# First softmax in halves, half of a halo mask and one weight cast moved to GpSimd, and four columns summed by TensorE alone, in the start of a fused dynamic convolution and max-out feed-forward kernel

## Chip, cores and metric

The kernel runs on one core of a Trainium2 chip. The metric is the device time of one execution in microseconds (us). The engines are called by the profile's names: PE is TensorE (PEld its weight loads), DVE is VectorE, ACT is ScalarE, POOL is GpSimd, SP is SyncE, which here only issues DMAs.

## What is computed

The input x is 8 x 4160 tokens of 192 numbers (33280 tokens in all), in 8 heads of 24. A causal convolution over 7 tokens has a softmax of its own for every token and head; its result goes through a max-out layer of width 1024.

```python
def _attn_ref(x, weight_gen):            # weight_gen: B, S, 8 heads, 7 taps
    w = np.exp(weight_gen - max over taps)
    w = w / (np.sum(w, axis=-1, keepdims=True) + 1e-09)
    x_pad = 6 zero tokens ahead of each sequence
    return einsum('bshk,bskhg->bshg', w, x_unf)      # 7 neighbouring tokens
...
h1 = x @ w1                               # 192 -> 1024
h2 = x @ w2
g = np.maximum(h1, h2)
return g @ w_out                          # 1024 -> 192
```

## The kernel before

**Layout.** Each of the 128 partitions holds 260 consecutive tokens, here called columns. Sixteen columns make a batch (17 batches, the last with 4 columns). Batches 0 and 1 are cut into pieces of 4 columns, later ones into pieces of 8. A piece is a unit of the feed-forward part.

**Softmax of a batch.** `load_wg` loads the 7 x 8 raw weights of each column. `exp_sum` (ACT, L127) takes the exponential, `red` (DVE, L139) sums over the taps, `ln` (ACT, L142) takes the logarithm of the sum, `shift` (DVE, L147) subtracts it from the raw weights, and `weights` (ACT, L158) takes the exponential again, which is the normalised softmax, into `en_t` in bf16, every value twice.

**Convolution of a piece.** `mul` (DVE, L173) multiplies seven shifted copies of x with the weights into `m_t` (7 taps side by side). For batches 2 and later, `adds` has three DVE additions (L189, L195, L198) that leave the sum in `y_t`; a DMA transposes it into `yt`. For the first eight units (batches 0 and 1) the sum over taps and the transposition are done on PE: `sum_transpose(u)` (L239) multiplies the taps with an identity and accumulates them in PSUM, and ACT copies the result into `yt` (L246). With all 7 taps that is 84 matmuls. Where the DVE has first done the first of its additions, `adds(b, o, True)`, four tiles `LEFT` are left and it is 48 matmuls. Units 0, 1 and 3 have all seven taps; units 2 and 4 to 7 are of the LEFT kind.

**Feed-forward.** The max-out is computed as h1 + relu(h2 - h1). `w_diff` (DVE subtractions L551 and L555, and three copies into other partitions by an engine that it is given) makes the difference of the two weights in two halves. `hid_tile` (PE, L275) makes a tile of the hidden layer, `relu` (ACT, L285) rectifies it into `rd_t`, and PE multiplies with `moe_w_out` (L315). The h1 part is folded: w1 is transposed on PE (`w1_transposed`, L580, from the bf16 copies `w1E` of rows 0 to 127 and `w1T` of rows 128 to 191), copied by ACT (L640), multiplied with w_out (`w10_product`, L622) and copied (`w10_copies`, L634); PE then adds `yt` times that product to the output (L327). ACT evacuates it (L371) and SP stores it.

**The start.** Everything is issued in a hand-written order; each engine runs its own instructions in that order. x for columns 0 to 7 and the weights come by SP's queue in f32. The six tokens ahead of each partition's first one (the halo, 1152 numbers) come in two DMAs, of SP and of POOL; where a sequence begins, the halo is zeroed by a multiplication with the mask `msk`, on ACT (L536). x of columns 0 to 3 is cast by DVE (L540), of columns 4 to 7 by ACT (L547). POOL copies one number per partition as a gate (L560), so that its own loads start only after the first halves of the weights have landed; then come its loads of x and w_out. `load_x(1, 0, 8)` issues the load of batch 1's first 8 columns and then a DMA (L121) that copies the last six columns of batch 0 to batch 1's halo; it waits for columns 12 to 15 of batch 0. PE runs 30 dummy matmuls (`keep_warm`, L592) until the first `sum_transpose`.

**Later.** From batch 2 on, `transpose(u)` issues the DMA transpose, and POOL copies one number of its result into `gate` (L215) ahead of its next loads. DVE runs a batch or two ahead of PE.

Of the kernel before, what the change touches and what calls it, by code (L numbers as in the profile page):

```python
# [23 lines left out]
def kernel(  # L24
# [83 lines left out]
                        ap=[[CPP * WGC, P], [1, n * WGC]]),  # L108
        )

    def load_x(b, o, n):

        if b not in xb_ts:
            xb_ts[b] = pxb.tile([P, (16 + PAD) * D], BF16, name="xb_t", tag="xb")
        nc.gpsimd.dma_start(  # L115
            out=xb_ts[b][:, (PAD + o) * D:(PAD + o + n) * D],
            in_=bass.AP(tensor=x.tensor, offset=(BATCHES[b][0] + o) * D,
                        ap=[[CPP * D, P], [1, n * D]]),
        )
        if b > 0 and o == 0:  # L120
            nc.gpsimd.dma_start(out=xb_ts[b][:, 0:PAD * D],  # L121
                                in_=xb_ts[b - 1][:, 16 * D:(16 + PAD) * D])


    def exp_sum(b):
        e_ts[b] = pe_.tile([P, BATCHES[b][1] * WGC], FP32, name="e_t", tag="e")
        nc.scalar.activation(out=e_ts[b], in_=wg_ts[b], func=AF.Exp)  # L127

    def part(b, i, of):

        n = BATCHES[b][1]
        h0, h1 = n * i // of * H, n * (i + 1) // of * H
        return slice(h0, h1), h0 * K, [[K, h1 - h0], [1, K]]

    def red(b, i=0, of=1):
        if i == 0:
            s_ts[b] = psm.tile([P, BATCHES[b][1] * H], FP32, name="sum_t", tag="sum")
        hs, at, ap = part(b, i, of)
        nc.vector.reduce_sum(out=s_ts[b][:, hs], in_=_sub(e_ts[b], at, ap), axis=AX.X)  # L139

    def ln(b):
        nc.scalar.activation(out=s_ts[b], in_=s_ts[b], func=AF.Ln)  # L142

    def shift(b, i=0, of=1):
        hs, at, ap = part(b, i, of)
        w_t = _sub(wg_ts[b], at, ap)
        nc.vector.tensor_tensor(out=w_t, in0=w_t, in1=_sub(s_ts[b], hs.start, [[1, hs.stop - hs.start], [0, K]]),  # L147
                                op=ALU.subtract)
# [15 lines left out]
    def mul(b, o):  # L164

        n = dict(pieces(b))[o]
        if n == 4 and b < 2:
            m_out = _sub(m_t, K * o * D, [[64, 2], [P, K * 6], [1, 64]])
            x_in = _sub(xb_ts[b], o * D, [[2 * D, 2], [D, K], [1, 2 * D]])
        else:  # L170
            m_out = m_t[:, K * o * D:K * (o + n) * D]
            x_in = _sub(xb_ts[b], o * D, [[D, K], [1, n * D]])
        nc.vector.tensor_tensor(  # L173
            out=m_out, in0=x_in,
            in1=_sub(en_ts[b], o * WGC * 2, [[2, K * n * H], [0, G // 2], [1, 2]]),
            op=ALU.mult,
        )

    def adds(b, o, first=False, beside=lambda i, of: None):


        w = dict(pieces(b))[o]
        n = w * D

        def taps(at, step, cnt):
            return _sub(m_t, K * o * D + at * n, [[step * n, cnt], [1, w * D]])

        beside(0, 3)
        nc.vector.tensor_tensor(out=taps(0, 1, 3), in0=taps(0, 1, 3), in1=taps(3, 1, 3), op=ALU.add)  # L189
        if first:  # L190
            return
        beside(1, 3)
        if b not in y_ts:
            y_ts[b] = py.tile([P, 16 * D], BF16, name="y_t", tag="y")
        nc.vector.tensor_tensor(out=taps(0, 2, 2), in0=taps(0, 2, 2), in1=taps(1, 5, 2), op=ALU.add)  # L195
        beside(2, 3)

        nc.vector.tensor_tensor(  # L198
            out=_sub(y_ts[b], o * D, [[64, 2], [P, 3 * w // 2], [1, 64]]),
            in0=taps(0, 1, 1), in1=taps(2, 1, 1), op=ALU.add,  # L200
        )
# [28 lines left out]
    def sum_transpose(u, taps=range(K)):  # L230

        b, o, n = UNITS[u]
        assert n == 4
        yps = ps["r" if "r" in ps else "o"].tile([P, 1024], FP32, name="yps", tag="op")
        for k in range(6):
            for t in taps:
                for r in range(2):
                    at = (K * o + t * n) * D + k * P
                    nc.tensor.matmul(  # L239
                        yps[:, r * 512 + k * 64:r * 512 + (k + 1) * 64],  # L240
                        lhsT=m_t[half(r), at:at + P], rhs=ident[half(r), half(r)],
                        start=(k == 0 and t == taps[0]), stop=(t == taps[-1]),
                        skip_group_check=True,
                    )
        yt = pyt.tile([P, 8 // 2 * 3 * P], BF16, name="yt", tag="yt")
        nc.scalar.copy(out=_sub(yt, 0, [[64, 2], [P, 6], [1, 64]]),  # L246
                       in_=_sub(yps, 0, [[512, 2], [64, 6], [1, 64]]))
        yt_ts[u] = yt
# [33 lines left out]
    def relu(rd, t0, n):  # L282

        (hd, at), k = hd_at[t0], rd_at[t0][1]
        nc.scalar.activation(out=rd[:, k * 1024:(k + n) * 1024], in_=hd[:, at:at + n * 1024],  # L285
                             func=AF.Relu)
# [124 lines left out]
    def room(g):  # L411

        t0, n = GROUPS[g]
        if "c" in ps:
            ab = ps["ab"].tile([P, 2048], FP32, name="hd2", tag="ab")
            for t in range(t0, t0 + n - 1):
                hd_at[t] = ab, (t - t0) * 1024
            hd_at[t0 + n - 1] = ps["c"].tile([P, 1024], FP32, name="hd1", tag="c"), 0
        else:
            for t in range(t0, t0 + n):  # L420
                hd_at[t] = ps["h"].tile([P, 1024], FP32, name="hdp", tag="hd"), 0
        rd = prd.tile([P, 3 * 1024], BF16, name="rd_t", tag="rd")
        for t in range(t0, t0 + n):
            rd_at[t] = (rd, t - t0)
        return rd
# [8 lines left out]
    def hidden(g, now=(), between=lambda: None, beside=lambda: None, ahead=lambda: None):  # L434


        t0, n = GROUPS[g]
        rd = room(g)
        for t in range(t0, t0 + n - 1):
            hid_tile(t)  # L440
        if now:
            out_room(now, "ab" if n == 1 and "ab" in ps else None)
            last = out_first(now)
        if len(now) > 2:
            relu(rd, t0, n - 1)
        else:
            for t in range(t0, t0 + n - 1):
                relu(rd, t, 1)
        if now:
            go = relay(last)  # L450
        hid_tile(t0 + n - 1)
        if len(now) > 2:
            beside()
        relu(rd, t0 + n - 1, 1)
        ahead()
        if now:
            out_second(now, go)
            evac(now[0] // 2, len(now) // 2)
        between()
        if len(now) <= 2:  # L460
            beside()
# [25 lines left out]
    with tc.tile_pool(name="pstage", bufs=1) as pstage:  # L487
# [23 lines left out]
        def load_w(h):  # L511
            for kind, r0, nr in (("E", 0, P), ("T", P, 64)):
                for wi, wsrc in enumerate((moe_w1, moe_w2)):
# [14 lines left out]
        nc.vector.tensor_single_scalar(out=msk_i, in_=msk_i, scalar=1, op=ALU.min)  # L528
        nc.vector.tensor_copy(out=msk, in_=msk_i)
        nc.vector.tensor_copy(out=ident, in_=ident_f)  # L530
        exp_sum(0)
        red(0)
        ln(0)
        shift(0)
        xb_ts[0] = pxb.tile([P, (16 + PAD) * D], BF16, name="xb_t", tag="xb")
        nc.scalar.activation(out=xb_ts[0][:, 0:PAD * D], in_=xs[:, 0:PAD * D], func=AF.Copy,  # L536
                             scale=msk[:, 0:1])
        for o in (0, 4, 8, 12):
            weights(0, o)
# [8 lines left out]
        def w_diff(h, copy):  # L548

            c0, c1, c2 = (slice(s * F + h * HF, s * F + (h + 1) * HF) for s in range(3))  # L550
            nc.vector.tensor_tensor(out=wd[:, c0], in0=ws["E", 1][:, c0], in1=ws["E", 0][:, c0],  # L551
                                    op=ALU.subtract)
            copy(out=wd[64:P, c2], in_=wd[0:64, c0])
            copy(out=wd[0:64, c1], in_=wd[64:P, c0])
            nc.vector.tensor_tensor(out=wd[0:64, c2], in0=ws["T", 1][:, c0], in1=ws["T", 0][:, c0],  # L555
                                    op=ALU.subtract)
            copy(out=wd[64:P, c1], in_=wd[0:64, c2])
# [6 lines left out]
            out=wo[:, :].rearrange("p (f d) -> p f d", d=D),  # L564
            in_=bass.AP(tensor=moe_w_out.tensor, offset=0, ap=[[D, P], [P * D, FCH], [1, D]]),
        )
        load_x(1, 0, 8)
        load_wg(2, nc.gpsimd)
        load_x(1, 8, 8)
        load_wg(3, nc.gpsimd)  # L570
# [18 lines left out]
        def keep_warm(times):  # L589

            for _ in range(times):
                nc.tensor.matmul(warm[:, 0:512], lhsT=ident, rhs=_sub(ident, 0, [[0, 4], [1, P]]),  # L592
                                 start=True, stop=True, skip_group_check=True)

        keep_warm(30)
        w_diff(0, nc.scalar.copy)
        sum_transpose(0)
        keep_warm(6)
# [1 line left out]


        nc.scalar.copy(out=w1["E"][:, HF:F], in_=ws["E", 0][:, HF:F])
        hidden(0)
        nc.scalar.copy(out=w1["T"], in_=ws["T", 0])
        w_diff(1, nc.vector.tensor_copy)
        mul(0, 8)
        sum_transpose(1)
        exp_sum(1)
        red(1)
        adds(0, 8, True)  # L610
        hidden(1)
        ln(1)
        shift(1)
# [27 lines left out]
        weights(1, 0)  # L641
        mul(1, 0)
        adds(1, 0, True)
        sum_transpose(2, LEFT)
        load_x(2, 0, 16)
        load_wg(4, nc.gpsimd)
        rd = room(3)
# [138 lines left out]
```

The softmax here doesn't subtract the row's maximum and nothing guards it: scores larger than these inputs give would overflow.

## Time and profile before

| | us |
|---|---|
| median of 7 runs (413.42 to 414.62) | 414.4 |
| the profiled execution, its own time | 414.4 |
| its span, first to last instruction | 412.5 |
| busy in the span: PE / DVE / ACT / POOL | 397.6 / 376.9 / 359.2 / 76.6 |
| granted TensorE clock, mean | 0.998 of full |

A row of the timeline is: start, duration, engine and source line, operation, written tile <- read tiles, shapes as partitions x elements, count, and in brackets the engine's idle time before it with what ended it. Records of neighbouring ACT and DVE instructions overlap by some 0.1 us, so a step in a row of instructions is the difference of two starts. In the list of waits a row gives the total, the count and the longest.

### The profile page before, as it was taken

The numbers are of one execution on the slowest core, as the hardware profiler recorded it, in microseconds if no ns is written. First come the engines' busy times: TensorE is split into PE (matmuls) and PEld (weight loads), VectorE is DVE, ScalarE is ACT, GpSimd is POOL, SyncE is SP. The second block draws the span as 40 slices with busy tenths as digits, with TensorE's granted clock in tenths as the row PEclk, the third lists the DMA queues.
The fourth block names the chain that finished last, engine by engine and source line by source line (L and its number), as shares of the span: only waits on it lengthen the run. The fifth ranks groups of instructions, "written<-read, shape, count | busy, mean of one in ns | idle before, by whom it ended". The sixth has DMA issues, their size and how long they took to land.

```text
span 412.5 us, 15844 instructions
## 1 busy us (share of the span) xinstructions
PE 397.6 (96%) x7276; PEld 316.5 (77%) x7276; DVE 376.9 (91%) x218; ACT 359.2 (87%) x425; POOL 76.6 (19%) x102
## 2 busy tenths in 40 slices
PE   7989999999999999999999999999999999999994
PEld 2678999677777787777777787777777677777794
DVE  5999999999999999999999999999999999999000
ACT  5999998989999988999988999989998888888771
POOL 1510102212211232222012222120122121210000
PEclk9999999999999999999999999999999999999999
DMA  8975535775657885864896497588648748654513
GB/s 242 258 183 159 146 79 133 174 160 140 168 118 162 196 164 129 224 178 101 133 258 162 97 261 178 71 246 185 127 103 239 168 74 228 155 85 144 147 77 118
DMA packets 60242, 65.68 MB, mean 159 GB/s; under 512 B 47601, under 2 KB 48497, under 8 KB 60176
## 3 DMA queue, kind: packets, MB, share of 16 engines
q1 hardware_dynamic: 51904, 40.47, 36.6%
q0 software_dynamic: 8128, 24.11, 28.3%
q8 instruction: 57, 0.93, 0.9%
q10 hardware_dynamic: 144, 0.10, 0.1%
q14 instruction: 9, 0.07, 0.1%
HBM read 35.96 MB, written 25.56 MB: 149 GB/s over the span
## 4 chain that ended last, share of the span: by engine, by line
DVE 69%; PE 17%; ACT 5%; issue 4%; DMA 3%; SPq 1%; DVEq 0%
DVE m_t L173 35%; DVE m_t L189 15%; DVE m_t L195 10%; PE op_ps L315 8%; PE hd L275 6%; DVE sum_t L139 3%; DVE y_t L198 3%; DVE wg_t L147 3%; ACT rd_t L285 2%; DMA ws1T<-in_moe_w_dram 2%; PE op_ps L327 2%; DMA yt<-y_t 1%; ACT yt L246 1%; PE hdp L275 1%; ACT e_t L127 1%
## 5 line engine op out<-in xcount | busy, mean ns | idle before, releaser
L285 ACT ACTIVATE rd_t<-hd 128x1024 bf16<-128x1024 f32 (+1 forms) x206 | 234.7, 1189 | 28.3 <-PE hd L275 26.7
L315 PE MATMUL op_ps<-wo,rd_t 64*128 64x192 bf16 x4160 | 210.6, 243 | 0.1
L315 PEld LDWEIGHTS <-rd_t 64*128 64x128 bf16 x4160 | 180.9, 94 | 15.7 <-ACTq L348 0.3
L275 PE MATMUL hd<-yt,wd 64*128 64x512 bf16 (+1 forms) x1584 | 187.5, 360 | 2.4 <-ACT rd_t L285 1.9
L173 DVE TENSOR_TENSOR m_t<-xb_t,en_t 128x10752 bf16<-128x10752 bf16 (+1 forms) x37 | 187.6, 5071 | 0.3 <-ACT en_t L158 0.3
L275 PEld LDWEIGHTS <-wd 64*128 64x128 bf16 x1776 | 94.3, 94 | 44.6 <-issue 3.9
L215 POOL CAST gate<-yt 128x1 f32<-128x1 bf16 x29 | 41.0, 1414 | 273.3 <-DMA yt<-y_t 273.3
L189 DVE TENSOR_TENSOR m_t<-m_t 128x4608 bf16<-128x4608 bf16 (+1 forms) x34 | 79.6, 2340 | 0.1
L371 ACT COPY o_t<-op_ps 128x384 f32<-128x384 f32 (+1 forms) x99 | 57.2, 590 | 13.8 <-PE op_ps L315 13.6
L327 PE MATMUL op_ps<-w,yt 64*128 64x192 bf16 x780 | 55.5, 243 | 1.4 <-ACT w L634 0.7
L327 PEld LDWEIGHTS <-yt 64*128 64x128 bf16 x780 | 38.4, 94 | 17.7 <-issue 2.2
L195 DVE TENSOR_TENSOR m_t<-m_t 128x3072 bf16<-128x3072 bf16 (+1 forms) x29 | 50.1, 1726 | 0.1
L158 ACT ACTIVATE en_t<-wg_t 128x896 bf16<-128x896 f32 (+2 forms) x45 | 35.2, 818 | 0.0
L198 DVE TENSOR_TENSOR y_t<-m_t 128x1536 bf16<-128x1536 bf16 (+1 forms) x29 | 27.3, 942 | 0.5
L361 DVE COPY o_t<-op_ps 128x192 f32<-128x192 f32 x1 | 0.4, 358 | 25.7 <-ACT o_t L361 25.7
L147 DVE TENSOR_TENSOR wg_t<-wg_t,sum_t 128x280 f32<-128x280 f32 (+4 forms) x45 | 22.0, 489 | 0.4 <-ACT sum_t L142 0.4
L139 DVE TENSOR_REDUCE sum_t<-e_t 128x64 f32<-128x448 f32 (+2 forms) x30 | 19.6, 655 | 2.4 <-ACT e_t L127 2.4
L115 POOL DMA_DIRECT2D xb_t<-in_x_dram x32 | 17.2, 539 | 22.9 <-DVE m_t L173 22.3
L127 ACT ACTIVATE e_t<-wg_t 128x896 f32<-128x896 f32 (+1 forms) x17 | 16.0, 939 | 2.4 <-DMA wg_t<-in_weight_gen_dram 2.4
L285 ACT ACTIVATE rd_t<-hdp 128x1024 bf16<-128x1024 f32 x16 | 15.9, 1033 | 1.0 <-PE hdp L275 1.0
L275 PE MATMUL hdp<-yt,wd 64*128 64x256 bf16 x192 | 12.8, 269 | 0.8 <-ACT rd_t L285 0.5
L592 PE MATMUL warm<-ident 128*128 128x512 bf16 x36 | 10.6, 461 | 3.0 <-DVE ident L530 3.0
(46 smaller groups left out, 75.3 us busy)
## 6 DMA issues: line engine op xcount, KB each, us to landing
out_dram<-o_t SPq DMA_DIRECT2D x28, 768.0 KB, 4.5
xb_t<-in_x_dram POOLq DMA_DIRECT2D x28, 384.0 KB, 4.8
wg_t<-in_weight_gen_dram POOLq DMA_DIRECT2D x14, 448.0 KB, 5.8
xb_t<-xb_t POOLq DMA_DIRECT2D x16, 288.0 KB, 5.0
out_dram<-o_t SPq DMA_DIRECT2D x8, 384.0 KB, 3.0
wg_t<-in_weight_gen_dram SPq DMA_DIRECT2D x2, 448.0 KB, 4.7
xs<-in_x_dram SPq DMA_DIRECT2D x2, 384.0 KB, 6.3
xb_t<-in_x_dram POOLq DMA_DIRECT2D x1, 768.0 KB, 8.6
```

The lines of the kernel that those rows point to most:

```text
L147: nc.vector.tensor_tensor(out=w_t, in0=w_t, in1=_sub(s_ts[b], hs.start, [[1, hs.stop - hs.start], [0, K]]), op=ALU.subtract)
L158: nc.scalar.activation(out=_sub(en_ts[b], (o * WGC + j * N * K) * 2, [[2 * N, K], [2, N], [1, 2]]), in_=_sub(wg_ts[b], (o * H + j * N) * K ...
L173: nc.vector.tensor_tensor(out=m_out, in0=x_in, in1=_sub(en_ts[b], o * WGC * 2, [[2, K * n * H], [0, G // 2], [1, 2]]), op=ALU.mult,)
L189: nc.vector.tensor_tensor(out=taps(0, 1, 3), in0=taps(0, 1, 3), in1=taps(3, 1, 3), op=ALU.add)
L195: nc.vector.tensor_tensor(out=taps(0, 2, 2), in0=taps(0, 2, 2), in1=taps(1, 5, 2), op=ALU.add)
L198: nc.vector.tensor_tensor(out=_sub(y_ts[b], o * D, [[64, 2], [P, 3 * w // 2], [1, 64]]), in0=taps(0, 1, 1), in1=taps(2, 1, 1), op=ALU.add,)
L215: nc.gpsimd.tensor_copy(out=gate, in_=yt[:, 0:1])
L275: nc.tensor.matmul(hid_out(t, f, j), lhsT=wd[half(j), s * F + f * P:s * F + (f + 1) * P], rhs=_sub(yt_ts[u][half(j), :], (s + j) % 3 * P, ...
L285: nc.scalar.activation(out=rd[:, k * 1024:(k + n) * 1024], in_=hd[:, at:at + n * 1024], func=AF.Relu)
L315: return nc.tensor.matmul(op_out(c), lhsT=rd[half(r), k * 1024 + at:k * 1024 + at + P], rhs=wo[half(r), f * D:(f + 1) * D], start=False, s ...
L327: nc.tensor.matmul(op_out(c + j), lhsT=yt_ts[u][half(j), (3 * i + (s + j) % 3) * P:(3 * i + (s + j) % 3 + 1) * P], rhs=w10[half(j), s * D: ...
L371: nc.scalar.copy(out=_sub(o, c % 24 * D, [[D, len(qs)], [h * D, 2], [1, D]]), in_=_sub(tile_, at + (qs[0] - p) * D, [[D, len(qs)], [512, 2 ...
```

## The change

The first batch's softmax runs as two halves of eight columns: `exp_sum`, `red`, `ln` and `shift` are issued twice each. The halo is masked half by POOL (576 of the 1152 numbers) and half by ACT. The cast of w1's last 64 rows (`w1T`, 64 x 1024) goes from ACT to POOL, between the load of batch 1's first columns and the DMA that copies its halo. `adds(0, 8, True)` is dropped and `sum_transpose(2)` sums all seven taps on PE. Three dummy matmuls fewer run in `keep_warm`. The exponential of batch 1 moves between the two relus of `hidden(0)` (which is written out), and `red(1)` moves ahead of `mul(0, 8)`; `w_diff(1)` and `sum_transpose(1)` keep their places on their engines.

```diff
-    def load_x(b, o, n):
+    def load_x(b, o, n, amid=lambda: None):
...
+        amid()
         if b > 0 and o == 0:
             nc.gpsimd.dma_start(out=xb_ts[b][:, 0:PAD * D],
                                 in_=xb_ts[b - 1][:, 16 * D:(16 + PAD) * D])
...
-    def exp_sum(b):
-        e_ts[b] = pe_.tile([P, BATCHES[b][1] * WGC], FP32, name="e_t", tag="e")
-        nc.scalar.activation(out=e_ts[b], in_=wg_ts[b], func=AF.Exp)
+    def exp_sum(b, i=0, of=1):
+        if i == 0:
+            e_ts[b] = pe_.tile([P, BATCHES[b][1] * WGC], FP32, name="e_t", tag="e")
+        w = BATCHES[b][1] * WGC // of
+        nc.scalar.activation(out=e_ts[b][:, i * w:(i + 1) * w], in_=wg_ts[b][:, i * w:(i + 1) * w], func=AF.Exp)
...
-    def ln(b):
-        nc.scalar.activation(out=s_ts[b], in_=s_ts[b], func=AF.Ln)
+    def ln(b, i=0, of=1):
+        s_t = s_ts[b][:, part(b, i, of)[0]]
+        nc.scalar.activation(out=s_t, in_=s_t, func=AF.Ln)
...
-        exp_sum(0)
-        red(0)
-        ln(0)
-        shift(0)
+        for step in (exp_sum, red, ln, shift):
+            for i in range(2):
+                step(0, i, 2)
         xb_ts[0] = pxb.tile([P, (16 + PAD) * D], BF16, name="xb_t", tag="xb")
-        nc.scalar.activation(out=xb_ts[0][:, 0:PAD * D], in_=xs[:, 0:PAD * D], func=AF.Copy,
+        HP = PAD * D // 2
+        nc.gpsimd.tensor_scalar(out=xb_ts[0][:, 0:HP], in0=xs[:, 0:HP], scalar1=msk[:, 0:1], scalar2=None,
+                                op0=ALU.mult)
+        nc.scalar.activation(out=xb_ts[0][:, HP:2 * HP], in_=xs[:, HP:2 * HP], func=AF.Copy,
                              scale=msk[:, 0:1])
...
-        load_x(1, 0, 8)
+        load_x(1, 0, 8, lambda: nc.gpsimd.tensor_copy(out=w1["T"], in_=ws["T", 0]))
...
-        keep_warm(30)
+        keep_warm(27)
...
         nc.scalar.copy(out=w1["E"][:, HF:F], in_=ws["E", 0][:, HF:F])
-        hidden(0)
-        nc.scalar.copy(out=w1["T"], in_=ws["T", 0])
+        rd = room(0)
+        hid_tile(0)
+        relu(rd, 0, 1)
+        exp_sum(1)
+        hid_tile(1)
+        relu(rd, 1, 1)
         w_diff(1, nc.vector.tensor_copy)
+        sum_transpose(1)
+        red(1)
         mul(0, 8)
-        sum_transpose(1)
-        exp_sum(1)
-        red(1)
-        adds(0, 8, True)
         hidden(1)
         ln(1)
         shift(1)
...
-        sum_transpose(2, LEFT)
+        sum_transpose(2)
```

## Prediction

> **What bounds the kernel now.** First the page: PE and DVE are both nearly full.
>
> ```profile
> PE 397.6 (96%) x7276; PEld 316.5 (77%) x7276; DVE 376.9 (91%) x218; ACT 359.2 (87%) x425; POOL 76.6 (19%) x102
> ```
>
> Which of the two sets the end is seen in the chain that ended last. It is DVE's row of operations up to 342 us, one transposing DMA, and then PE alone.
>
> ```profile
> 330.71 5.75 DVE m_t L173
> ...
> 341.74 0.88 DVE y_t L198
> 342.76 4.42 DMA yt<-y_t
> 347.21 0.82 PE hd L275 x6
> ```
>
> The list of waits says how tight that handover is: in the whole run PE waited once for a transposed tile, for 0.4 us.
>
> ```profile
> PE hd L275 <- DMA yt<-y_t: 0.4, 1, 0.4
> ```
>
> In the middle of the run DVE needs 23.66 us for 16 columns (L173 starts at 58.61 and 82.27 in the chain), 1.48 us a column; PE in its tail repeats after 8.64 us for 6 columns (L315 at 352.75, 361.39, 370.02), 1.44 a column. PE starts behind DVE and catches up just before the end. So if the start brings DVE forward by D and PE by E, the end moves by the smaller of D and E + 0.4. Neither alone is enough.
>
> Next the start, on DVE's timeline. From 8.73 us each row begins where the one before it ends: whatever is saved or lost here is kept to 342.
>
> ```profile
> 5.40 1.09 DVE L139 TENSOR_REDUCE sum_t<-e_t 128x128 f32<-128x896 f32 x1 [2.44 <-ACT e_t L127]
> 6.86 1.09 DVE L147 TENSOR_TENSOR wg_t<-wg_t,sum_t 128x896 f32<-128x896 f32 x1 [0.38 <-ACT sum_t L142]
> 7.87 0.55 DVE L540 CAST xb_t<-xs 128x768 bf16<-128x768 f32 x1
> 8.73 2.96 DVE L173 TENSOR_TENSOR m_t<-xb_t,en_t 128x5376 bf16<-128x5376 bf16 x1 [0.30 <-ACT en_t L158]
> ...
> 12.81 2.94 DVE L173 TENSOR_TENSOR m_t<-xb_t,en_t 128x5376 bf16<-128x5376 bf16 x1
> 15.67 0.68 DVE L551 TENSOR_TENSOR wd<-ws1E,ws0E 128x512 bf16<-128x512 f32 x1
> ...
> 21.92 1.35 DVE L189 TENSOR_TENSOR m_t<-m_t 128x2304 bf16<-128x2304 bf16 x1
> 23.18 1.08 DVE L147 TENSOR_TENSOR wg_t<-wg_t,sum_t 128x896 f32<-128x896 f32 x1
> ```
>
> ACT's timeline has the halo mask, the cast that waits for x, and the cast that leaves ACT:
>
> ```profile
> 6.76 1.26 ACT L536 ACTIVATE xb_t<-xs,msk 128x1152 bf16<-128x1152 f32 x1
> ...
> 11.36 0.83 ACT L547 CAST xb_t<-xs 128x768 bf16<-128x768 f32 x1 [0.39 <-DMA xs<-in_x_dram]
> ...
> 17.77 1.03 ACT L604 CAST w1T<-ws0T 64x1024 bf16<-64x1024 f32 x1
> ```
>
> Last, POOL's timeline, with DVE's row of the same time in the second fence. A cast of one number takes 0.18 us where DVE runs a reduction (206.44), but 1.75 where DVE runs a multiplication of two SBUF tensors: it ends 0.05 after it (64.32, 64.27).
>
> ```profile
> 2.09 0.24 POOL masks.py:197 MEMSET ident_f<- 128x128 f32 x1
> 2.40 0.29 POOL masks.py:199 TENSOR_SCALAR_AFFINE_SELECT ident_f<-ident_f 128x128 f32<-128x128 f32 x1
> ...
> 62.57 1.75 POOL L215 CAST gate<-yt 128x1 f32<-128x1 bf16 x1 [16.68 <-DMA yt<-y_t]
> ...
> 206.44 0.18 POOL L215 CAST gate<-yt 128x1 f32<-128x1 bf16 x1 [10.93 <-DMA yt<-y_t]
> ```
>
> ```profile
> 58.52 5.75 DVE L173 TENSOR_TENSOR m_t<-xb_t,en_t 128x10752 bf16<-128x10752 bf16 x1
> ```
>
> **First softmax in halves.** Its weights land at 4.40. ACT's slope is 0.81 ns a number (steps of 0.85 for 896, 0.31 for 224), so half an exponential is a row of 0.58: 4.42 to 5.00, the second to 5.49. A reduction of 448 is a row of 0.61: 5.03 to 5.64, the second from 5.56 to 6.18. The logarithms end at 5.95 and 6.48, both ahead of DVE; the subtractions (0.61 each) run 6.10 to 6.71 and 6.64 to 7.25. Before they ended at 7.95: 0.7 earlier. What is late next is the halo and x: the two halo DMAs landed at 6.36 and 6.73, x of the first columns at 7.45. ACT's half of the mask is 1.26 - 576 x 0.81 ns = 0.79, 6.76 to 7.55; its first two `weights` end at 8.22, so that is the earliest for `mul(0, 0)`.
>
> **POOL's half of the mask.** No row shows a wide cast on POOL. One number costs 0.18; the memset gives 1.08 ns a further number ((0.24 - 0.10) / 127), the affine select 0.86 ((0.29 - 0.18) / 127); I take 0.97, so 576 numbers are 0.74. If all of the select's 0.29 went by size it would be 1.3. It can begin at 6.75, finds DVE in the second subtraction, begins at 7.25 and ends at 7.99. DVE's cast L540 comes next. If POOL holds it up, `mul(0, 0)` starts at 8.47, else at 8.22; gain 0.26 or 0.5, with the slow POOL -0.3. I take 0.26. `mul(0, 4)` also needs L547, whose x lands at 11.34 as before (done 12.19); DVE comes to it at 12.55, so it costs nothing.
>
> **The w1T cast on POOL.** From ACT it takes a step of 0.99 (17.77 to 18.76). On POOL it stands behind the gate, three loads and one of w_out, which ended at 14.23 and will at 13.9; its source landed at 13.66. It meets `mul(0, 4)`, running to 15.49, and waits for that, as the gate rows do. Then it reads 64 x 1024 numbers: 0.18 + 1023 x 0.97 ns = 1.17, bounds 1.06 and, by size alone, 2.3. DVE's next instruction is L551, which reads two SBUF tensors. That POOL waits for such an instruction is shown; that DVE waits for POOL is not, since one number is too short to show it. So the cost to DVE lies between nothing and the whole cast. I take the whole, because what excludes the two from each other in one order is likely to in the other: L551 starts at 16.66 in place of 15.41 (15.67 - 0.26), cost 1.25. The Trainium skill, SBUF - State Buffer, section "Who interferes with whom", speaks against this part of the change in the same sense: a VectorE instruction with two SBUF inputs and a GpSimd instruction that reads SBUF exclude each other for a whole instruction, whichever starts first. By that rule the sum is the one with 1.25; without it, the one with nothing. Behind the cast on POOL's queue stands the halo DMA L121, which waited until 18.81 for columns 12 to 15: cover of over 2 us to the cast's end at 16.66. `w1T` is read on PE near 20.5.
>
> **`adds(0, 8, True)` removed.** DVE's step is 23.18 - 21.92 = 1.26, all on its continuous row. PE's 36 more matmuls cost (1.40 - 0.88) / 36 each by the two L239 rows, 0.52 together, in a stretch where PE idled 2 of 17 us (19 to 36). The three dummies (0.30 each) give back 0.91, ending PE's warm-up near 11.1, ahead of `mul(0, 0)`'s end: no cost.
>
> **The order around it.** `red(1)` now needs `exp_sum(1)`, done about 17.5 between the two relus; DVE comes later in both cases. `ln(1)` stands behind the relus of tiles 2 and 3, near 21.5; `shift(1)` comes at 22.9: no stall.
>
> **Sum for DVE.** 0.26 + 1.26 - 1.25 = 0.27 earlier at `shift(1)` and from there on.
>
> **Sum for PE.** `w_diff(1)` ends at 18.05 + 1.0 = 19.05, and tiles 2 and 3 need it (PE came at 18.55). Tile 2 ends at 19.7, its relu starts at 19.75 (20.31 before); tile 4's relu then waits for PE, 22.05 (22.32). The w1t copies start at 23.85 (24.12), `sum_transpose(2)` starts after `mul(0, 8)` at 22.95 and ends at 24.3, w10 follows tiles 6 and 7 at 25.6 (25.70), its copies end at 29.0 (29.27), and PE goes on 0.25 earlier. E + 0.4 = 0.65 exceeds 0.27, so DVE sets the end. From the profiled 414.4 (span 412.5 and 1.9 around it; also the median of the runs) it is 414.1. A measurement of this kernel tells about 0.2%, 0.8 us, from no change, so this counts as within it.
>
> **Rivals.** *POOL doesn't hold DVE up.* DVE gains 0.5 + 1.26 = 1.75; PE gains what ACT loses of work, 0.99, so E + 0.4 = 1.4 sets the end: 413.0. For it: the gate casts left no trace on DVE's next row. Against: one number is no test.
> *POOL is slow and holds the pair of engines for long; slower.* With 2.3 us for the cast and 1.3 for the mask DVE stands at -0.3 + 1.26 - 2.4 = -1.4: 415.8. With the mask as taken, the change turns to a loss once the cast holds DVE beyond 1.5 us, and beyond 2.35 it is a loss of over 0.8. For it: only tiny POOL casts are timed here. Against: memset and select both show about 1 ns a number.
> *PE's instructions come late.* PE has two stalls of 0.8 us inside `sum_transpose`, at 18.48 and 36.60, that the profile puts down to "issue"; 36 more quick matmuls could add one in PE's start, E = -0.5 and the end near 414.5: no change.
>
> **How the numbers follow.** DVE held up by about 1.2: 0.47, time 413.4 to 414.9 by the bounds of mask and cast (1.06 to 1.8). Not held up: 0.28, 412.7 to 413.3. Slow POOL: 0.18, 415.2 to 416. Late instructions: 0.07. The range 412.7 to 415.5 leaves out most of the slow case. Faster by over 0.2%: the second case and a short cast, 0.34; slower: the slow case and a little, 0.20; within: 0.46.
>
> **What would show it.** Right: a row of POOL for w1T of 1 to 1.3 us beginning or ending where `mul(0, 4)` ends, L551 some 1.2 us later after `mul(0, 4)` than its length says, `shift(1)` near 22.9, PE's transposed-tile wait still there near 347. Wrong: L551 unmoved behind `mul(0, 4)` and `shift(1)` near 21.5 (first rival), a POOL row above 2 us (second), or a PE gap above 0.5 us in 20 to 36 that is new (third).

## The result, and the profile after

The changed kernel takes 412.63 us (median of 22 runs) beside 413.91 for the kernel before (58 runs): the ratio on record is 0.9976 [0.997, 0.9982], a gain of 1.0 us (0.74 to 1.24); the plain difference of the two medians is 1.28. The gain of 0.24% is just over the 0.2% at which the prediction put its border between faster and no change, and the interval (0.18 to 0.30%) takes in that border. On the 414.4 from which the prediction counted, it is 413.4: inside its range, but 0.7 below the forecast. The median itself, 412.63, lies just under the range's lower end of 412.7.

The profiled execution has a span of 410.6. Of the 1.9 us between the two spans, 0.98 stands between the last matmuls of the two kernels, which start at 406.83 and 405.85; the other 0.88 lies behind them, in the final stores (below). The profiled execution of before, 414.4, is one of its longer ones. First the page: the busy times barely moved.

```profile
PE 396.8 (97%) x7309; PEld 316.1 (77%) x7309; DVE 376.6 (92%) x219; ACT 357.9 (87%) x426; POOL 82.9 (20%) x104
```

What moved is the chain that ended last. Before, it was DVE's row up to 342 us; now it is mostly PE, and DVE has 1% of it.

```profile
PE 83%; ACT 10%; issue 3%; DMA 2%; DVE 1%; SPq 1%; DVEq 0%; ACTq 0%
```

DVE's timeline of the changed kernel shows the start (L177 was L173, L557 was L551, L151 was L147):

```profile
8.79 2.96 DVE L177 TENSOR_TENSOR m_t<-xb_t,en_t 128x5376 bf16<-128x5376 bf16 x1 [0.61 <-POOL xb_t L540]
...
15.74 0.68 DVE L557 TENSOR_TENSOR wd<-ws1E,ws0E 128x512 bf16<-128x512 f32 x1
16.45 1.01 DVE L559 COPY wd<-wd 64x512 bf16<-64x512 bf16 x1
17.48 0.29 DVE L560 COPY wd<-wd 64x512 bf16<-64x512 bf16 x1
...
22.70 1.09 DVE L151 TENSOR_TENSOR wg_t<-wg_t,sum_t 128x896 f32<-128x896 f32 x1
```

And POOL's timeline has the two operations that it was given:

```profile
6.80 1.96 POOL L540 TENSOR_SCALAR xb_t<-xs,msk 128x576 bf16<-128x576 f32 x1 [4.09 <-DVE wg_t L151]
...
14.30 3.01 POOL L573 CAST w1T<-ws0T 64x1024 bf16<-64x1024 f32 x1
```

DVE's sum can be read off. The subtractions of the two halves end at 7.16, 0.79 earlier than before, but `mul(0, 0)` starts 0.06 later (8.79, 8.73), since it waits 0.61 for POOL's mask. The copy L559 takes 1.01 where its twin L560 takes 0.29: it was held up for 0.72 by POOL's cast. The cast itself takes 1.03 by itself (e7), so of its 3.01 it spent some 2 waiting for the multiplication and the subtraction ahead of that copy. The removed addition is worth its 1.26. So -0.06 - 0.72 + 1.26 = 0.48, and `shift(1)` does start 0.48 earlier (22.70, 23.18).

PE goes the other way. At 29 us it is 0.51 ahead (its first L331, L327 before, starts at 28.80 and 29.32). But its first long hidden tile starts at 49.49, at 49.14 before: 0.35 later, although DVE is ahead. PE's timeline shows why:

```profile
34.86 0.83 PE L279 MATMUL hdp<-yt,wd 64*128 64x256 bf16 x12 [0.90 <-issue]
```

It stops 0.90 in front of a hidden tile, with nothing outstanding that the profile shows, and ACT idles 1.45 for that tile (its relu starts at 35.73). Before, the stop of 0.74 stood inside `sum_transpose(4)`, where nobody waited for it:

```profile
36.60 0.81 PE L239 MATMUL yps<-ident,m_t 64*128 64x64 bf16 x43 [0.74 <-issue]
```

It is one and the same place. When the matmuls of the PE timeline are counted, 607 of them stand ahead of the stop in both kernels, and the change puts 33 more in the program ahead of that place (36 more of `sum_transpose(2)`, 3 dummies fewer). In the 14 profiles of this document there are 31 stops of PE by "issue" over 0.15 us. All stand behind 223, 351, 479, 607, 991 or 1119 matmuls: 128 apart, or a multiple of it. The page's row for instruction transfers, the same in both kernels, fits that:

```profile
q8 instruction: 57, 0.93, 0.9%
```

57 packets for 7309 matmuls are one for every 128, each of 0.93 MB / 57 = 16 KB. A matmul and its weight load make 256 instructions of 128 pairs. The traces have the time of each packet too: all 31 stops end 1.23 to 1.60 after the last packet before them has been transferred (in the changed kernel 33.48 and 34.86, before 35.21 and 36.60). So the place of a stop follows from the count. Its length is what is left of that time when PE gets there, and varies: the program of the kernel before has 0.74 behind 607 matmuls in this profile, 0.24 in a second one (e13) and none over 0.15 in e7, whose PE instructions are the same.

The Trainium skill, Runtime: NRT & Kernel Launch, section "Instruction fetch mechanics", has the same size (blocks of 16 KiB, 256 instructions, fetched by a DMA queue of the engine's own); it calls the cost of crossing a block mostly hidden. That agrees with 31 stops for the some 57 packets of each of 14 profiles; where it isn't hidden, it is up to 1.60 us here (e2).

So PE is 0.35 late at 49 us and still 0.46 late at 304 to 321. It is ahead from 325 on, and by 0.98 from 348 to the end. Most of that turn of 1.44 is in the kernel before: there PE stopped at two units, for 0.84 and 0.43, for which the changed kernel has no stop. PE's timeline of before:

```profile
323.61 1.47 PE L275 MATMUL hd<-yt,wd 64*128 64x512 bf16 x12 [0.84 <-ACT rd_t L285]
...
347.21 0.82 PE L275 MATMUL hd<-yt,wd 64*128 64x512 bf16 x6 [0.43 <-DMA yt<-y_t]
```

The first is put down to ACT, but POOL's timeline of before shows that the transposed tile had only just come: the gate that reads the same tile starts in the same moment, after a wait for the DMA.

```profile
323.60 1.05 POOL L215 CAST gate<-yt 128x1 f32<-128x1 bf16 x1 [9.76 <-DMA yt<-y_t]
```

The tiles came late because their transposing DMAs took longer than the others. The DMA view of before, from 319.0 to 323.5 (a queue with packets, MB and share; then the tile, its queue and us to landing):

```profile
q8 instruction: 1, 0.02, 1.9%
...
yt<-y_t SPq DMA_TRANSPOSE x1, 4.4
```

The unit after it, issued near 331, took 3.6, with no q8 row in its window; the one issued at 342.76 took 4.42, again with one packet of q8. In the changed kernel the one that follows DVE's row at 342, from 342.2 to 346.0, had no q8 row:

```profile
q1 hardware_dynamic: 1616, 0.69, 73.1%
...
yt<-y_t SPq DMA_TRANSPOSE x1, 3.7
```

Over 14 profiles (both kernels and all experiments), for units issued after 250 us: 85 tiles had an instruction packet start between 0.3 us before their issue and 3.6 after it, and took 4.14 in the median, 67 of them over 3.9. Of the 85 others, with a median of 3.68, one took over 3.9 (4.03). The changed kernel has late tiles too (issued at 294.95, 5.32; at 318.61, 4.12), but PE comes to these units later than the tiles.

The end of the program, behind the last matmul, changed in the same way. The DMA view of before, from 405.7 to 411.2, has a packet of q8 among the last stores, and the changed kernel, from 404.7 to 409.4 (second fence), has none:

```profile
q8 instruction: 1, 0.02, 1.1%
...
out_dram<-o_t SPq DMA_DIRECT2D x1, 768.0 KB, 4.4
out_dram<-o_t SPq DMA_DIRECT2D x1, 192.0 KB, 3.9
```

```profile
out_dram<-o_t SPq DMA_DIRECT2D x1, 768.0 KB, 3.3
out_dram<-o_t SPq DMA_DIRECT2D x1, 192.0 KB, 2.6
```

From the start of the last matmul to the end of the span it is 5.67 us before and 4.79 in the changed kernel. Over the 14 profiles, the six with a packet among the last stores (before, e1, e7, e11, e12, e13) have 5.54 to 5.87 there, the eight without 4.77 to 4.79. The time of each profiled execution exceeds its span by 1.8 to 1.9, so this part counts in the time. Against the two other profiles of PE's program before, e13 and e7, the last matmul of the changed kernel is 0.51 and 0.37 earlier, and the end behind it 0.84 and 0.75 shorter: against these, the larger part of the gain lies behind the last matmul.

### The profile page after: what moved, and what is told of

It reads as the page before. It is cut to its first block, busy times and chain, and to the rows that moved or that the text cites. A ratio compares the mean times of both kernels' runs of the same rounds, so it can differ in the third digit from the quotient of the medians.

```text
span 410.6 us, 15917 instructions
## 1 busy us (share of the span) xinstructions
PE 396.8 (97%) x7309; PEld 316.1 (77%) x7309; DVE 376.6 (92%) x219; ACT 357.9 (87%) x426; POOL 82.9 (20%) x104
## 4 chain that ended last, share of the span: by engine, by line
PE 83%; ACT 10%; issue 3%; DMA 2%; DVE 1%; SPq 1%; DVEq 0%; ACTq 0%
PE op_ps L319 38%; PE hd L279 36%; PE op_ps L331 7%; ACT rd_t L289 6%; DMA ws1T<-in_moe_w_dram 2%; ACT en_t L162 1%; PE hdp L279 1%; ACT o_t L375 1%; ACT yt L250 0%; ACT e_t L130 0%; SPq L518 0%; ACT w1t L648 0%; DVE wd L557 0%; DVE wd L561 0%; ACT w L642 0%
## 5 line engine op out<-in xcount | busy, mean ns | idle before, releaser
L177 DVE TENSOR_TENSOR m_t<-xb_t,en_t 128x10752 bf16<-128x10752 bf16 (+1 forms) x37 | 187.5, 5071 | 0.6 <-POOL xb_t L540 0.6
L219 POOL CAST gate<-yt 128x1 f32<-128x1 bf16 x29 | 42.2, 1455 | 271.5 <-DMA yt<-y_t 271.5
L193 DVE TENSOR_TENSOR m_t<-m_t 128x4608 bf16<-128x4608 bf16 (+1 forms) x33 | 78.2, 2371 | 0.1
L331 PE MATMUL op_ps<-w,yt 64*128 64x192 bf16 x780 | 55.5, 243 | 1.4 <-ACT o_t L375 1.4
L331 PEld LDWEIGHTS <-yt 64*128 64x128 bf16 x780 | 38.4, 94 | 18.1 <-issue 2.7
L151 DVE TENSOR_TENSOR wg_t<-wg_t,sum_t 128x280 f32<-128x280 f32 (+5 forms) x46 | 22.1, 481 | 0.0
L130 ACT ACTIVATE e_t<-wg_t 128x896 f32<-128x896 f32 (+2 forms) x18 | 16.1, 898 | 2.3 <-DMA wg_t<-in_weight_gen_dram 2.3
L598 PE MATMUL warm<-ident 128*128 128x512 bf16 x33 | 9.3, 445 | 3.0 <-DVE ident L534 3.0
```

Source lines behind the costliest of these rows:

```text
L177: nc.vector.tensor_tensor(out=m_out, in0=x_in, in1=_sub(en_ts[b], o * WGC * 2, [[2, K * n * H], [0, G // 2], [1, 2]]), op=ALU.mult,)
L219: nc.gpsimd.tensor_copy(out=gate, in_=yt[:, 0:1])
L331: nc.tensor.matmul(op_out(c + j), lhsT=yt_ts[u][half(j), (3 * i + (s + j) % 3) * P:(3 * i + (s + j) % 3 + 1) * P], rhs=w10[half(j), s * D: ...
```

## The experiments

Two theories competed first. A: the end still follows DVE's row, now earlier. B: it follows PE's row, and what DVE gains beyond that brings nothing. Later expectations also speak of the program's place against its instruction packets (they call them pages), which decides where PE stops and which tiles come late, and of the load of x for batch 2 as the cause of PE's stop near 35 (D). Ratios are to the kernel before.

**e1: the removed addition put back.**

```diff
         mul(0, 8)
+        adds(0, 8, True)
...
-        sum_transpose(2)
+        sum_transpose(2, LEFT)
```

> The changed kernel with adds(0, 8, True) back on DVE and sum_transpose(2) of the LEFT kind again (48 matmuls). DVE then stands 1.26 us later than in the changed kernel (1.26 - 0.48 = 0.78 later than before the change) from shift(1) to the end; PE has 36 matmuls less. Theory A, DVE sets the end: PE's matmuls wait again for transposed tiles near 300 to 347 us, and the time is 0.8 to 1.3 us above the changed kernel, that is near or up to 0.5 above the kernel before. Theory B, PE's own row sets the end since the change (its chain is 83% PE): the time is the changed kernel's or up to 0.5 lower.

415.9, ratio 1.0057 [1.0043, 1.007]. It is 3.3 us above the changed kernel, where DVE's loss of 1.26 alone was expected to cost that or nothing: neither theory had so much. With 36 matmuls fewer the packets are back nearly where they were before; the tiles of the units issued near 320.5 and 344.2 took 5.38 and 4.94, and with DVE also late PE waited for both (list of waits: total, count, longest):

```profile
PE hd L279 <- DMA yt<-y_t: 2.0, 2, 1.9
```

In its profile DVE's last addition near 342 is 1.93 later than in the changed kernel (343.11, 341.18), the tile behind it took 1.27 longer, and the last matmul comes 2.96 later; the end behind it is 0.84 longer, with a packet among the last stores again. So when tiles are late, DVE's row sets the end, and the late tile costs on top of it. The run also shows an order that the changed kernel doesn't: here POOL's cast begins ahead of the subtraction L557, which has two SBUF inputs and is held up for 0.85.

```profile
16.15 1.53 DVE L557 TENSOR_TENSOR wd<-ws1E,ws0E 128x512 bf16<-128x512 f32 x1
```

**e2: the cast of w1T moved beside the reduction.** A gate on the last copy of `w_diff(1)` stands ahead of the cast; batch 1's halo copy and the later loads of POOL come behind it.

```diff
+        nc.gpsimd.tensor_copy(out=gate[64:P, :], in_=wd[64:P, F + HF:F + HF + 1])
+        nc.gpsimd.tensor_copy(out=w1["T"], in_=ws["T", 0])
```

> The changed kernel with POOL's cast of w1T put behind a gate on the last copy of w_diff(1), so that it runs beside the reduction red(1); the DMA of batch 1's halo and the loads behind it move with it, about 0.5 us. If POOL's cast takes about 0.9 us by itself and holds up only DVE's copies (in the changed kernel L557, two SBUF inputs, kept its 0.68 us, and the copy L559 behind it took 1.01 in place of 0.29), the copies take 0.29 again, a reduction is not held up, and DVE is 0.6 to 0.75 us earlier from mul(0, 8) on. Rival: the cast takes 1.5 us by itself (15.81 to 17.31), lasts beyond the reduction and holds up mul(0, 8) by about 0.5: DVE gains 0.2 or less. In time, theory A (DVE sets the end) gives 0.4 to 0.7 us less than the changed kernel, theory B (PE) what PE gains at its wait for w_diff(1), 0.5, or nothing where PE's instruction stalls take it.

413.41, ratio 0.9996 [0.9987, 1.0005]: no gain. POOL's timeline has the cast by itself:

```profile
18.60 1.03 POOL L615 CAST w1T<-ws0T 64x1024 bf16<-64x1024 f32 x1
```

The copies are back at 0.29, and DVE is 0.65 to 0.8 ahead of before in the start, `mul(0, 8)` being held for 0.25. PE is 1.43 behind before at 51 us, since its stop has grown:

```profile
35.92 0.83 PE L278 MATMUL hdp<-yt,wd 64*128 64x256 bf16 x12 [1.60 <-issue]
```

DVE's lead did not last: it is 0.65 until 164 us, 0.15 behind a wait of 0.40 for ACT's logarithm near 170, and gone from 247 on. So the run doesn't test what a lead of DVE is worth at the end. It does show PE's row setting it: the last matmul is 0.99 later than in the changed kernel (406.84, 405.85), with no tile late near 342 (3.67). B's number, no loss against the changed kernel, missed too.

**e3: the half of the mask on DVE.**

```diff
-        nc.gpsimd.tensor_scalar(out=xb_ts[0][:, 0:HP], in0=xs[:, 0:HP], scalar1=msk[:, 0:1], scalar2=None,
+        nc.vector.tensor_scalar(out=xb_ts[0][:, 0:HP], in0=xs[:, 0:HP], scalar1=msk[:, 0:1], scalar2=None,
```

> The changed kernel with POOL's half of the halo mask on DVE. In the changed kernel mul(0, 0) waited 0.61 us for POOL's mask, which took 1.96 us (6.80 to 8.76). DVE is idle from 7.16 to 7.48 there; 576 numbers from f32 to bf16 should take about 0.45 by the row of the cast L546 (0.55 for 768), so mul(0, 0) starts near 8.05 in place of 8.79, and mul(0, 4), which needs ACT's cast of x that lands at 11.43, near 12.3 in place of 12.87: DVE gains 0.55 from there. Theory A: 0.4 to 0.55 us less time than the changed kernel. Theory B: 0 to 0.2.

412.52, ratio 0.998 [0.9971, 0.999]. DVE's timeline: the mask takes 0.51 instead of 1.96, and `mul(0, 0)` no longer waits for it.

```profile
6.99 0.51 DVE L540 TENSOR_SCALAR xb_t<-xs,msk 128x576 bf16<-128x576 f32 x1
...
8.21 2.96 DVE L177 TENSOR_TENSOR m_t<-xb_t,en_t 128x5376 bf16<-128x5376 bf16 x1
```

DVE's row is 0.58 earlier than in the changed kernel in the start and 0.35 at 342 (340.83, 341.18), and the time is the same: the last matmul is even 0.11 later, with PE's first long hidden tile 0.22 later (49.71). PE stops 1.34 ahead of 35.08. A falls; B holds.

**e4: e2 and e3 together.**

> Both edits together: POOL's cast beside red(1), the half mask on DVE. DVE's gains add: 1.1 to 1.3 us earlier than in the changed kernel at shift(1), unless ln(1) on ACT (21.43 there) now holds shift(1) up. Theory A: 0.9 to 1.3 us less time than the changed kernel (near 411.7 where the kernel before takes 413.9). Theory B: PE has only its own gain, at most 0.5, and the time is 0 to 0.5 lower.

412.61, ratio 0.9985 [0.9973, 0.9998]. DVE is 1.70 ahead of before in the start, PE 0.61 behind at 50 us, and the time is that of the changed kernel within the intervals. Here too DVE had to wait for ACT near 170:

```profile
169.72 0.45 DVE L150 TENSOR_TENSOR wg_t<-wg_t,sum_t 128x280 f32<-128x280 f32 x1 [0.63 <-ACT sum_t L145]
```

At 342 it is 0.78 ahead of before and 0.31 ahead of the changed kernel. These 0.31 are worth nothing; what a lead of 1.2 would be worth at the end is not shown, since no run kept it. The profile is 0.82 shorter than that of e2, which is the difference of their PE rows at 50 us (49.75, 50.57).

**e6: PE later, in the kernel before.** `sum_transpose(7)` runs twice.

```diff
-        for k in range(6):
+        for k in [*range(6)] * (2 if u == 7 else 1):
```

> The kernel before the change with the 48 matmuls of the eighth sum_transpose issued twice (the second pass overwrites the first), so that PE is some 0.8 us later from 49 us on and DVE is where it was. Theory C, before the change the transposed tiles that come from DVE set the end, and PE had spare time (its waits for such tiles add up to about 1.4 us near 323 and 347): the time is the kernel before's within 0.3. Rival, PE alone sets the end before the change too: 0.8 us more.

413.78, ratio 1.0002 [0.9994, 1.0011]. It tells little: idle time took up most of the added work, and PE came only 0.04 later at 62 us and 0.30 at 320. It also shifts the packets by 48 matmuls: other tiles are late (5.27 for the one issued at 330.7), and the last stores are free of a packet (4.78 behind the last matmul, where the kernel before has 5.67), so that the equal time doesn't tell for theory C.

**e7: POOL's operations alone.** In the kernel before, on scratch data, while POOL is idle at the start.

```diff
+        nc.gpsimd.memset(sc_f, 0.5)
+        nc.gpsimd.tensor_scalar(out=sc_b[:, 0:576], in0=sc_f[:, 0:576], scalar1=ident_f[:, 0:1], scalar2=None, op0=ALU.mult)
+        nc.gpsimd.tensor_copy(out=sc_b[0:64, :], in_=sc_f[0:64, :])
```

> The kernel before with three POOL instructions more on scratch data between 2.7 and 5.5 us, where DVE runs nothing (its reduction at 5.4 reads one tensor): a memset of 1024 numbers, the masking form for 576 numbers from f32 to bf16, and the cast of 64 x 1024 from f32 to bf16. If the cast's 3.0 us in the changed kernel was mostly waiting for DVE, it takes 0.9 to 1.1 alone; if POOL is slow by itself, 1.5 to 3. The mask, 1.96 in the changed kernel: 0.6 to 0.8 alone if waiting made it long, 1.5 or more if its form is slow.

413.53. POOL's timeline:

```profile
3.70 1.73 POOL L530 TENSOR_SCALAR m_t<-m_t,ident_f 128x576 bf16<-128x576 f32 x1
5.49 1.03 POOL L531 CAST m_t<-m_t 64x1024 bf16<-64x1024 f32 x1
```

The mask costs 1.73 / 576 = 3.0 ns a number, the cast 1.0. The mask's form is slow by itself; the cast is not, and its 3.01 in the changed kernel is mostly waiting.

**e8: only the addition dropped, from the kernel before.**

```diff
-        adds(0, 8, True)
...
-        sum_transpose(2, LEFT)
+        sum_transpose(2)
```

> The kernel before the change with adds(0, 8, True) dropped and all seven taps of unit 2 summed on PE, nothing else. DVE is 1.26 us earlier to the end, more than with the whole change (0.48). If the end is the later of DVE's tiles and PE's row, PE decides: its row is as in the changed kernel or later, because the 36 matmuls move its instruction stalls, and the time is near the changed kernel's, 0.5 to 1.2 us below the kernel before. Rival, what DVE gains is what counts: 1.26 below.

413.07 (12 runs), ratio 0.9986 [0.9976, 0.9995]: this one edit brings 0.6 of the 1.0 us. The tile issued near 344 took 3.68, and the end behind the last matmul 4.78. Its profile is of its slowest execution (414.43), in which x landed at 9.21 in place of 7.45 and PE came to its first long hidden tile at 51.63. The edit does two things: it frees 1.26 us of DVE, and it shifts the packets by 36 matmuls.

**e10: the packets alone.** The kernel before, with 36 matmuls more in `sum_transpose(0)` (their sum is overwritten by the full pass behind them) and two dummies fewer; DVE has all its work.

```diff
+        passes = [(k, t) for k in range(6) for t in taps]
+        if u == 0:
+            passes = [(k, t) for k in range(6) for t in (0, 1, 2)] + passes
...
-        keep_warm(6)
+        keep_warm(4)
```

> The kernel before the change with 36 short matmuls more in the first sum_transpose (an extra pass over three taps, overwritten by the full one) and two dummies fewer in the warm-up behind it, so that PE's times stay within 0.1 us and only the position of its later instructions moves by 34 matmuls, as in the change (33). DVE has nothing changed. If the position of the instruction pages is what put PE 0.35 us later at 50 us in the changed kernel, the stall of about 1 us near 36 us moves from sum_transpose(4) to tile 9 here too, and PE is 0.6 to 1.1 us later at 50 us than before. The time stays within 0.4 us of the kernel before, as DVE's tiles set it. Rival, the position does nothing: PE is at its old times.

413.0 (11 runs), ratio 0.9985 [0.9976, 0.9994]. A program with 34 matmuls more on PE and no work less on any other engine is 0.62 us faster. The expectation had the place of the stop right, but not the time, which was to stay within 0.4 of before. Its profile is of the changed kernel's kind: the stop comes behind the same 607 matmuls, no tile is late near 342 (3.7), the end behind the last matmul takes 4.79, and DVE is gone from the chain that ended last.

```profile
PE 82%; ACT 12%; issue 2%; DMA 2%; SPq 1%; DVE 0%; DVEq 0%; ACTq 0%
```

```profile
35.00 0.25 PE L318 MATMUL op_ps<-wo,rd_t 64*128 64x192 bf16 x1 [0.83 <-issue]
...
49.70 1.49 PE L278 MATMUL hd<-yt,wd 64*128 64x256 bf16 x24 [0.19 <-ACT rd_t L288]
```

Its PE row starts the long hidden tiles 0.21 later than the changed kernel's (49.70, 49.49), which has the sign of what is left between the two; their intervals overlap.

**e9: the load of x for batch 2 cut in two.** On top of e3, its second half and the next weights' load wait for `mul(1, 8)`, so that less is in flight at PE's stop.

```diff
-        load_x(2, 0, 16)
-        load_wg(4, nc.gpsimd)
+        load_x(2, 0, 8)
...
+        nc.gpsimd.tensor_copy(out=gate, in_=m_t[:, K * 8 * D:K * 8 * D + 1])
+        load_x(2, 8, 8)
+        load_wg(4, nc.gpsimd)
```

> The kernel with the half mask on DVE (e3), and the load of batch 2's x cut in two: the first eight columns where they were, the other eight and the weights of batch 4 behind a POOL gate on mul(1, 8), near 39 us. In e3 and in the changed kernel PE stalls about 1 us near 35 us at tile 9 of the hidden layer while instruction pages arrive late beside that load, and ACT, which is full there, idles 1.45 us. Theory D, the load delays PE's instructions: the stall is under 0.4 us, PE is 0.6 to 1.0 us earlier at 50 us, and as PE sets the end in e3 the time is 0.5 to 1.0 below e3, near 411.8. Rival, the stall belongs to the page's place in the program and not to the load: no change against e3.

412.1 (5 runs), ratio 0.9965 [0.9953, 0.9977], the lowest time of all, though its interval overlaps that of the changed kernel. PE still stops for 1.11 behind 607 matmuls (at 34.38), so D isn't borne out. PE was 0.5 ahead of e3 at 33 us, before the moved load could act; its first long hidden tile starts at 49.03, 0.46 before that of the changed kernel, and its last matmul 0.30 before. What puts PE ahead is not shown.

**e11 and e12: the packets moved back by one whole packet.** The changed kernel and e9 get 100 short dummies in place of five long ones: 95 matmuls more, which with the 33 of the change make 128 more than before, one packet, so that the rest of the program lies against its packets as it did before.

```diff
-        keep_warm(6)
+        for _ in range(100):
+            nc.tensor.matmul(warm[:, 0:64], lhsT=ident[half(0), :], rhs=ident[half(0), half(0)],
+                             start=True, stop=True, skip_group_check=True)
+        keep_warm(1)
```

> The changed kernel with five of the six dummies behind the first sum_transpose replaced by 100 short ones (1.6 us in place of 1.2, where PE idles before the first hidden tile), so that PE has 256 instructions more than the kernel before the change: one whole page, and the pages begin at the same places of the program as before it. Theory, the places of the pages decide: PE's stall near 35 us is in sum_transpose(4) again, PE is 0.4 to 0.9 us earlier at 51 us than in the changed kernel, pages meet the transposing DMAs near 318 and 342 again, and PE waits there; the time is set by DVE and 0.3 to 0.7 below the kernel before, above the changed kernel's. Rival, PE's gain at 51 us counts: 0.4 to 0.9 below the changed kernel.

> The same shift of the pages in e9 (half mask on DVE, batch 2's x in two parts), where DVE is about 1.0 us earlier than before the change. If DVE's lead is enough even where pages meet the transposing DMAs, PE's row sets the end, 0.4 to 0.9 below e9: near 411.3. If not, DVE's tiles do: 412.3 to 412.9.

418.37, ratio 1.012 [1.0089, 1.0152], and 417.52, ratio 1.0097 [1.0074, 1.012]. The edit failed as a test of time: the dummies took 3.08 us, twice what was meant, PE came 1.5 late to its first hidden tile, and e11 has three stops over 1 us in the first 54 us (18.48, 28.40 and 53.95). What they do show: there is no stop near 35 any more, the late tiles are back (in e11 5.28 for the one issued at 322.0, 4.88 at 345.6), and so is the packet among the last stores (5.87 and 5.63 behind the last matmul).

**e13: the kernel before once more**, to see whether its late tiles are chance.

> The kernel before, unchanged, for a second profile of it. If the late transposed tiles follow from where PE's instruction pages lie, the DMAs issued near 319 and 343 us are again above 4.2 us from issue to landing, those near 307 and 331 near 3.7, and PE waits again at the same two units; if they are chance, they lie elsewhere.

413.78. The same two units are late (4.21 and 4.24), their neighbours are not (3.69 and 3.65), and PE waits for both again, 0.75 and 0.4. So which tiles are late is a property of the program. How late is not: in e7, with the same PE and DVE instructions, the two took 4.08 and 3.83. The two profiles of one program also show how far single profiles differ: here DVE is 0.28 earlier than in the first, and PE's first long hidden tile 0.58 earlier (48.56). The chain that ended last has DVE for 14% here (from 283 to 342 us) where the first has 69%; its end, DVE's row, the DMA and then PE, is the same.

**What sets the end, over all profiles.** In the six with the packets where they were (before, e1, e7, e11, e12, e13) the last matmul starts 59.64 to 59.66 after the landing of the tile that was issued between 342.4 and 345.7, whether that came at 346.56 or at 350.50: the tile sets the end. From the first long hidden tile to the last matmul it is 357.06 to 358.61 there. In the seven of the changed kernel's kind (after, e2, e3, e4, e8, e9, e10) that difference varies, 59.90 to 60.38, but the last matmul starts 356.24 to 356.52 after the first long hidden tile, whether that came at 49.03 or at 51.63: PE's row sets the end. e6, with other tiles late, is of neither kind.

## Why the prediction was right or wrong

**DVE's terms.** The removed addition was worth its 1.26. The halves of the softmax were to bring 0.26 and brought -0.06: the mask on POOL was priced at 0.74 from a memset and a select, and takes 1.96 (1.73 alone). The halves themselves came as forecast (7.16 for 7.25). The cast was priced well (1.17; 1.03 alone), and that POOL holds DVE up is shown, in both orders: it waited for the multiplication, then held a copy for 0.72, and in e1 a subtraction for 0.85. The section of the Trainium skill that the prediction named, SBUF - State Buffer, "Who interferes with whom", agrees for that subtraction. The price of 1.25 was too high, because the cast came behind the subtraction instead of ahead of it. Together D is 0.48 and not 0.27; the errors partly cancel, and e13 has a DVE row 0.28 earlier than the profile that the prediction read. That a lead of DVE is kept to 342 held for these 0.48, but not for the 0.65 of e2 or the 1.70 of e4.

**PE's term.** E was to be +0.25 and is -0.35 (-0.93 and -0.33 against e13 and e7). At 29 us PE was ahead as forecast, by 0.51. The step that failed is the last one of the sum for PE: it followed the waits for data and took the stop by "issue" as part of the place where it stood. It belongs to a count of instructions, and now fell in front of a tile for which ACT waited 1.45. The third rival had named this (a new stop, E = -0.5) at a chance of 0.07.

**The rule for the end.** "The smaller of D and E + 0.4" took 0.4 from the list of waits as all that PE lost to late tiles; a stop of 0.84 for the same cause stood under ACT's name. And it took a tile's way through the DMA as fixed, where it is 3.7 or 4.1 to 5.4. With E = -0.35 the rule gives an end 0.05 earlier; the last matmul came 0.98 earlier. The tile that had set the end landed 1.22 earlier (347.17, 345.95), 0.48 of it by DVE and the rest by a shorter DMA (4.42, 3.67); PE came later than the tile, and then its own row set the end.

**What stands behind the last matmul.** The sum took it as fixed: the end was to move as the last matmul does. It became 0.88 shorter (0.84 and 0.75 against e13 and e7), since no packet fell among the last stores. This is the term that the sum put at nothing without a reason, and against e13 and e7 it is the larger part of the gain.

**The sum.** The forecast of 414.1 was in the right direction and too small by 0.7, because the gain's main mechanism was not in it: with 33 matmuls more, the program lies differently against its instruction packets, so that the last stores and the tile near 342 go without one. e10 shows such a shift alone to be worth 0.62 [0.25, 0.99] of the 1.0. In its profile the end behind the last matmul is 0.75 to 0.88 shorter than in the three profiles of PE's program before (before, e7, e13), and the last matmul 0.08 to 0.69 earlier. What DVE's 0.48 added to that is not separated by any run. That the time fell into the range is luck as far as the mechanism goes: the range was made of prices for the mask and the cast. The rival without any hold on DVE came near in its time (413.0) and is wrong in its reason. Of the signs that the prediction named, the wait near 347 was to stay and is gone, and a new gap over 0.5 in 20 to 36 is there: both spoke against it. POOL's row of 3.01 is the second rival's sign, though some 2 of it was waiting. The third rival had that gap, but with no gain from it.

**Open.** Why some packets, the one at 607 matmuls in 11 of 14 profiles, come so late that PE stops, where most come unnoticed; why a transposing DMA takes 0.4 to 1.7 us longer, and the last stores some 0.8, with one packet of 16 KB in their time; and why e9 is lowest. Other shifts of the program than these were not tried, nor was the cast on ACT with the rest of the change.

## What to carry to other kernels

A change in the number of instructions ahead of a place moves every instruction packet behind it: before such a change is credited with the work that it saves, run a version that shifts the program and saves nothing. When a wait is small in the list, look whether another engine's wait for the same tile ends in the same moment; the profile puts a wait for several semaphores under one name only. Look at what follows the last matmul as well: here it held 0.75 to 0.88 us of the gain, and no step of the sum had gone there. And a gain on one engine counts only until the other one sets the end: here DVE was 0.58 and 1.22 us further ahead in the start, lost part of it in a wait for ACT, and the 0.3 that was left changed nothing.

## What the runs showed of the hardware

A transposing DMA with an instruction packet in its time took 4.14 in the median (85 tiles), without one 3.68 (85 tiles). From the last matmul to the end of the span it took 5.54 to 5.87 with a packet among the last stores (6 profiles), 4.77 to 4.79 without (8 profiles). PE's stops by "issue" ended 1.23 to 1.60 after a packet had been transferred (31 stops). POOL's multiplication by a value per partition took 3.0 ns a number, its cast 1.0. Short matmuls that all use one half of the rows took 30 ns each (e11: 100 in 3.08 us), while the `sum_transpose` row of before, 43 in 0.81, stands at up to 19; no run changes that one thing alone.
